# Softmax weights transposed by the DMA engines instead of TensorE, in a kernel of windowed attention and a feed-forward layer

## The chip, the cores and the metric

The program runs on one core of one Trainium2 chip. Five engines work side by side, each through its own list of instructions in order: TensorE (PE in the profile; its weight loads are PEld), VectorE (DVE), ScalarE (ACT), GpSimd (POOL) and SyncE (SP, which here does nothing but issue transfers). The metric is the device time of one execution in microseconds.

## The reference

Attention over a window of 128 positions with a linear bias by distance, for 8 batches of 8 heads, 576 positions and 64 elements a head; its output, one row of 512 for each of 4608 tokens, goes through a feed-forward layer of 2048 with an activation made of comparisons and a square.

```python
scores = scale * np.matmul(q, k.transpose(0, 1, 3, 2))
mask = (rel >= 0) & (rel < window)
scores = np.where(mask, scores + bias[None], -1000000000.0)
scores = scores - np.max(scores, axis=-1, keepdims=True)
attn = np.exp(scores)
attn = attn / (np.sum(attn, axis=-1, keepdims=True) + 1e-09)
return np.matmul(attn, v).astype(np.float32)
...
h = x @ w_in
g = np.where(pos, h, np.where(neg, 0.0, (h + beta) ** 2 / (4.0 * beta)))
return (g @ w_out).astype(np.float32)
```

## The kernel before

The 4608 tokens are cut into 12 chunks of 384 (CH), each of three blocks of 128. For each chunk the attention of 8 heads is done in 4 pairs, numbered p = 0 to 47 through the whole run, with heads m = 2p and 2p + 1. Then the feed-forward layer of that chunk runs in 16 steps, fc = 0 to 15. The attention of chunk c + 1 is woven into the feed-forward steps of chunk c, so that TensorE has matmuls of one while the other engines work on the other.

Products in float32 accuracy are made of float16 halves: a number is scaled, its rounded value is the high half, the rest the low half, and three matmuls (high by high, high by low, low by high) make one product. Chunks 0 and 1 are treated in plain float32 (LIGHT = 2), so 80 heads, in 40 pairs, take the path that the change touches.

A pair of heads passes these stages:

- scores_of_pair (L461) multiplies q and k on TensorE into PSUM banks named s_m_0 and s_m_2.
- soften adds the bias and takes the row maximum (L484, DVE), the exponential with its sums (L486, ACT), the sum's reciprocal (L493), folds the two window halves on each other (L497, DVE) and multiplies by the reciprocal (L498, DVE). The result ep_m is 128 queries by 384 (three blocks of 128 keys), float32, in SBUF. It has two buffers.
- weights_t turns each of the three blocks round, since the next matmul needs keys on the partitions: three float32 transposes on TensorE (L507) into a PSUM bank p_m. ACT writes the high half (L519) and DVE the low half (L520) from that bank into lu_m, which holds for each half six blocks of 128 by 128, the odd ones written here. POOL then makes of each odd block its part above and its part below the diagonal: L522 writes the even blocks, L524 rewrites the odd ones. lu has three buffers, so lu_m takes the place of lu_(m - 3), which the values of an earlier pair must have read.
- values_of_pair multiplies the weights of both heads with v (L564), 24 or 18 small matmuls into a bank x_p; L573 (ACT) and L574 (DVE) split the result into the halves that layer 1 reads.

The banks s, p and x share one pool of three PSUM banks (ps_a).

A feed-forward step is layer1 and layer2. layer1 makes 12 matmuls (L593 to L595) into a bank h; ACT makes u of it (L600), DVE makes g of u (L601) and of h (L602), ACT rounds g to gh (L609) and POOL subtracts for the low half gl (L610). layer2 runs two steps behind (LAG = 2), 9 matmuls (L625 to L627) into three banks acc; L627 reads gl. After step 15 ACT writes the rows out (L638) and SP stores them.

SP issues all transfers in order: the loads of q and k (L306, L307) and v (L379) of a pair, some five pairs ahead of their use, and the stores of the output.

The order on each engine isn't written out. The program hands the work to a scheduler in the order of a list of segments, in which for each pair stand: scores of p, the split of v, values of p - 1, weights_t(2p), the split of q and k of p + 1, weights_t(2p + 1). emit_attention spreads these over the half-steps of the feed-forward layer, and the scheduler then sets the order on every engine by its own reckoning of when each operand is ready and each buffer free.

Of the kernel before, what the change touches and what calls it, by code (L numbers as in the profile page):

```python
# [9 lines left out]
F16 = mybir.dt.float16  # L10
# [4 lines left out]
AF = mybir.ActivationFunctionType  # L15
ALU = mybir.AluOpType
# [4 lines left out]
def windowed_attention_then_ffn(  # L21
# [21 lines left out]
    V, S, G, T, DMA = nc.vector, nc.scalar, nc.gpsimd, nc.tensor, nc.sync  # L43
# [4 lines left out]
    P = 128  # L48
# [3 lines left out]
    NQB = 3  # L52
    CH = NQB * P
# [6 lines left out]
    TOP = 2.0 ** 14  # L60
# [8 lines left out]
    ap1 = ctx.enter_context(tc.tile_pool(name="ap1", bufs=1))  # L69
# [6 lines left out]
    def bank(name):  # L76
        return ps_a.tile([P, 4 * P], F32, name=name, tag="ps_a")


    ident = const.tile([P, P], F32, name="ident")  # L80
# [421 lines left out]
    def weights_t(m):  # L502

        ep = head[m]["ep"]
        pt = bank(f"p_{m}")[:, :CH].rearrange("r (i w) -> r i w", w=P)
        for i in range(NQB):
            T.transpose(pt[:, i, :], ep[:, i, :], ident)  # L507
        if m < LIGHT * H:
            lu = head[m]["lu"] = ap1.tile([P, 2 * NQB, P], F32, name=f"lu_{m}", tag="lu", bufs=3)
            own = lu[:, 1::2, :]  # L510
            ga = S.copy(own, pt)
            G.affine_select(out=lu[:, 0::2, :], in_=own, pattern=[[0, NQB], [-1, P]],
                            base=0, channel_multiplier=1, compare_op=ALU.is_gt, fill=0.0)
            gg = G.affine_select(out=own, in_=own, pattern=[[0, NQB], [1, P]],
                                 base=0, channel_multiplier=-1, compare_op=ALU.is_ge, fill=0.0)
            done_t[m] = [head[m]["held"].ins, ga.ins, gg.ins]
            return
        lu = head[m]["lu"] = ap1.tile([P, 2, 2 * NQB, P], F16, name=f"lu_{m}", tag="lu", bufs=3)
        ga = S.activation(lu[:, 0, 1::2, :], pt, AF.Copy, scale=TOP)  # L519
        gv = V.scalar_tensor_tensor(lu[:, 1, 1::2, :], pt, TOP, lu[:, 0, 1::2, :], ALU.mult, ALU.subtract)  # L520
        flat = lu.rearrange("p s i w -> p (s i) w")
        G.affine_select(out=flat[:, 0::2, :], in_=flat[:, 1::2, :], pattern=[[0, 2 * NQB], [-1, P]],  # L522
                        base=0, channel_multiplier=1, compare_op=ALU.is_gt, fill=0.0)
        gg = G.affine_select(out=flat[:, 1::2, :], in_=flat[:, 1::2, :], pattern=[[0, 2 * NQB], [1, P]],  # L524
                             base=0, channel_multiplier=-1, compare_op=ALU.is_ge, fill=0.0)
        done_t[m] = [ga.ins, gv.ins, gg.ins]
# [127 lines left out]
    def turn(m):  # L654
        segments.append([lambda: weights_t(m)])
        turned[m] = len(segments)
# [34 lines left out]
    for p in range(p8, NP):  # L691
        c, g = divmod(p, NPAIR)
        nc_, ng = divmod(p + 5, NPAIR)
        new = p + 5 < NP
        segments.append([lambda p=p: scores_of_pair(p, (0, 1))])
        if p == p8:
            segments.append([lambda p=p: behind(softened[p], lambda: reach_of(p + 4))])
        if new:
            segments.append([lambda p=p: behind(softened[p], lambda: reach_of(p + 5))])
        if new and ng == NPAIR - 1:  # L700
            segments.append([lambda nc_=nc_: level(nc_)])
        segments.append([lambda p=p: scores_of_pair(p, (2,))])
        if g == NPAIR - 1 and c + 1 < NCHUNK:
            segments.append([lambda c=c: near_of(c + 1)])
        segments.append([lambda p=p: split_v(p)] + ([lambda p=p: load_all(p + 6)] if p + 6 < NP else []))
        if p > p8:
            segments.append([lambda p=p: values_of_pair(p - 1)])
            if g == 0:
                ready.append(len(segments))
        if new and ng == NPAIR - 1:  # L710
            segments.append([lambda nc_=nc_: scale_all(nc_)])
        segments.append([lambda p=p: weights_t(2 * p)])
        if p + 1 < NP:
            segments.append([lambda p=p: split_qk(p + 1)])
        segments.append([lambda p=p: weights_t(2 * p + 1)])
# [98 lines left out]
    for i, ops in enumerate(ffn):  # L814
        c, r = divmod(i, STEPS)
# [37 lines left out]
```

## Time and profile before

| | |
|---|---|
| median of 3 runs | 983.93 us (983.66 to 986.0) |
| profiled execution | 983.55 us |
| span of the profiled execution | 981.8 us |
| mean granted TensorE clock | 0.989 of full |
| PE busy | 954.0 us, 97% |
| DVE, ACT, POOL busy | 74%, 62%, 36% |
| chain of work that ended last | PE 89%, DVE 4%, ACT 4%, DMA 1% |

The span runs from the first to the last instruction on the core; the execution's own time is 1.75 us longer. A busy PE is one whose matmuls overlap without a gap; since matmuls are pipelined, what one of them costs is read from the distance between the starts of two, not from the length of one. The granted clock is the share of full speed that TensorE had: 1.0 is 2.4 GHz, 0.5 is 1.2 GHz.

### The profile page before, as it was taken

To read this page: it belongs to the slowest core of one execution; us is meant where nothing else is said; L and a number is where in the kernel's file an instruction comes from. 1 tells how busy PE (TensorE), PEld (TensorE's weight loads), DVE (VectorE), ACT (ScalarE), POOL (GpSimd) and SP (SyncE) were. 2 spreads that over 40 slices of the span, in tenths; PEclk is the share of its full clock that TensorE was granted. 3 is DMA by queue.
4 is the path that set the end of the run, shared out by engine and by line. 5 is a ranking of instruction groups with operands and counts; after the bars stand their busy time and mean duration, and the time that the engine had idled before them with its cause. 6 is when DMAs were issued, how large, how long until landed. Compare 5 with 4: busy or idle time off the path is not lost.

```text
span 981.8 us, 17793 instructions
## 1 busy us (share of the span) xinstructions
PE 954.0 (97%) x6181; PEld 523.0 (53%) x6181; DVE 722.9 (74%) x2073; ACT 607.3 (62%) x1508; POOL 357.6 (36%) x464
## 2 busy tenths in 40 slices
PE   8699999998999999999999999999999999999998
PEld 5344545554555555555555555555555555555554
DVE  7888888887777886786786787687677786765332
ACT  6888767667557555666665765665666655544332
POOL 5322313334343334333434433533433443334221
PEclk9899999997999999999999999999999999999999
DMA  8557520021011111012111111112101000000000
GB/s 266 187 190 268 189 65 33 12 66 65 30 52 57 33 41 63 30 49 70 35 52 34 57 41 39 63 30 60 62 30 31 33 1 2 33 1 1 33 1 32
DMA packets 53289, 59.86 MB, mean 61 GB/s; under 512 B 3408, under 2 KB 42576, under 8 KB 53200
## 3 DMA queue, kind: packets, MB, share of 16 engines
q1 hardware_dynamic: 53056, 58.60, 18.6%
q8 instruction: 48, 0.79, 0.3%
q14 instruction: 41, 0.34, 0.1%
q10 hardware_dynamic: 144, 0.13, 0.0%
HBM read 49.28 MB, written 9.44 MB: 60 GB/s over the span
## 4 chain that ended last, share of the span: by engine, by line
PE 89%; DVE 4%; ACT 4%; DMA 1%; issue 1%; SPq 0%; POOL 0%; ACTq 0%; DVEq 0%; POOLq 0%
PE h L593 13%; PE h L595 12%; PE h L594 12%; PE acc L625 12%; PE acc L626 12%; PE acc L627 12%; PE s L461 5%; PE x L564 4%; PE p L507 3%; PE acc L622 3%; PE x L541 1%; ACT z L486 1%; ACT raw L183 1%; PE s L445 1%; DMA k<-in_k_dram 1%
## 5 line engine op out<-in xcount | busy, mean ns | idle before, releaser
L610 POOL TENSOR_TENSOR gl<-g,gh 128x384 f16<-128x384 f32 x176 | 167.6, 952 | 432.9 <-ACT gh L609 424.9
L601 DVE SCALAR_TENSOR_TENSOR g<-u,half 128x384 f32<-128x384 f32 x176 | 121.9, 693 | 156.8 <-ACT u L600 146.4
L609 ACT CAST gh<-g 128x384 f16<-128x384 f32 x176 | 89.6, 509 | 186.1 <-DVE g L602 104.3
L625 PE MATMUL acc<-wo,gh 128*128 128x512 f16 x528 | 200.3, 379 | 0.0
L626 PE MATMUL acc<-wo,gh 128*128 128x512 f16 x528 | 200.3, 379 | 0.0
L627 PE MATMUL acc<-wo,gl 128*128 128x512 f16 x528 | 196.5, 379 | 0.0
L600 ACT ACTIVATE u<-h,shift,fall 128x384 f32<-128x384 f32 x176 | 116.6, 665 | 99.8 <-PE h L595 99.6
L486 ACT ACTIVATE z<-z,nmax 128x256 f32<-128x256 f32 (+2 forms) x288 | 137.7, 480 | 35.0 <-DVE nmax L484 29.7
L593 PE MATMUL h<-x,wi 128*128 128x384 f16 x384 | 125.7, 329 | 3.1 <-DVE g L602 1.5
L593 PE MATMUL h<-xh,wi 128*128 128x384 f16 x384 | 124.8, 327 | 2.5 <-DVE g L602 2.5
L594 PE MATMUL h<-x,wi 128*128 128x384 f16 x384 | 126.0, 328 | 0.0
L595 PE MATMUL h<-x,wi 128*128 128x384 f16 x384 | 125.9, 328 | 0.0
L594 PE MATMUL h<-xl,wi 128*128 128x384 f16 x384 | 125.2, 326 | 0.0
L595 PE MATMUL h<-xh,wi 128*128 128x384 f16 x384 | 125.0, 326 | 0.0
L484 DVE CUSTOM_DVE_ANT_0 z<-s,near,z_of 128x256 f32<-128x256 f32 (+2 forms) x240 | 98.5, 460 | 33.8 <-PE s L461 33.6
L602 DVE SCALAR_TENSOR_TENSOR g<-h,gain,g 128x384 f32<-128x384 f32 x176 | 108.2, 615 | 3.9
L593 PEld LDWEIGHTS <-wi 128*128 128x128 f16 x768 | 75.1, 98 | 63.1 <-issue 7.1
L594 PEld LDWEIGHTS <-wi 128*128 128x128 f16 x768 | 75.3, 98 | 59.5 <-issue 7.3
L595 PEld LDWEIGHTS <-wi 128*128 128x128 f16 x768 | 75.2, 98 | 52.3 <-issue 4.0
L522 POOL TENSOR_SCALAR_AFFINE_SELECT lu<-lu 128x768 f16<-128x768 f16 x80 | 70.1, 890 | 64.1 <-DVE lu L520 63.7
L627 PEld LDWEIGHTS <-gl 128*128 128x128 f16 x528 | 51.5, 98 | 58.7 <-issue 0.4
L625 PEld LDWEIGHTS <-gh 128*128 128x128 f16 x528 | 51.6, 98 | 50.8 <-issue 0.8
(150 smaller groups left out, 1455.5 us busy)
## 6 DMA issues: line engine op xcount, KB each, us to landing
out_dram<-o SPq DMA_DIRECT2D x35, 256.0 KB, 2.1
raw<-in_moe_w_in_dram SPq DMA_DIRECT2D x16, 512.0 KB, 3.8
raw<-in_moe_w_out_dram SPq DMA_DIRECT2D x16, 512.0 KB, 4.7
vn<-in_v_dram SPq DMA_DIRECT2D x32, 256.0 KB, 2.8
qk<-in_q_dram SPq DMA_DIRECT2D x40, 192.0 KB, 2.4
qk<-in_k_dram SPq DMA_DIRECT2D x28, 256.0 KB, 2.8
vn<-in_v_dram SPq DMA_DIRECT2D x16, 192.0 KB, 2.6
qk<-in_k_dram SPq DMA_DIRECT2D x12, 192.0 KB, 2.6
```

The lines of the kernel that those rows point to most:

```text
L484: a = V.tensor_tensor_reduce(out=z[:, i, c0:], in0=pt[:, n, c0:], in1=r[:, c0:], op0=ALU.add, op1=ALU.min, scale=factor, scalar=3.0e38, ac ...
L486: b = S.activation(z[:, i, c0:], z[:, i, c0:], AF.Exp, bias=nmax[:, i:i + 1], scale=-1.0, accum_out=sm[:, i, 0:1])
L593: T.matmul(ph, wi[fc][:, 0, cc, :], xh, start=(cc == 0), stop=False)
L594: T.matmul(ph, wi[fc][:, 0, cc, :], xl, start=False, stop=False)
L595: T.matmul(ph, wi[fc][:, 1, cc, :], xh, start=False, stop=(cc == NCC - 1))
L600: first = S.activation(u, ph, AF.Relu, bias=shift[c] if c else quarter, scale=fall[c][:, col])
L601: V.scalar_tensor_tensor(g, u, half[c] if c else 0.5, u, ALU.min, ALU.mult)
L602: last = V.scalar_tensor_tensor(g, ph, gain[c][:, col] if c else fall[c][:, col], g, ALU.mult, ALU.max)
L610: G.tensor_tensor(gl, g, gh, ALU.subtract)
L625: T.matmul(a, gh[:, ts], wo[fc][:, 0], start=first, stop=False)
L626: T.matmul(a, gh[:, ts], wo[fc][:, 1], start=False, stop=False)
L627: T.matmul(a, gl[:, ts], wo[fc][:, 0], start=False, stop=last)
```

## The change

From chunk 2 on, weights_t splits ep_m where it stands: ACT writes the high half and DVE the low half into a new tile hl_m (128 queries by two halves by 384 keys, float16, two buffers). One transfer on SP's queue with a transpose, 128 x 768 elements, 192 KB, turns the six 128 x 128 blocks round and writes them into the odd blocks of lu_m. POOL's two instructions are as before. The three TensorE transposes and the bank p_m are gone from these heads; chunks 0 and 1 keep them.

```diff
--- before.py
+++ after.py
@@ -502,10 +502,10 @@
     def weights_t(m):
 
         ep = head[m]["ep"]
-        pt = bank(f"p_{m}")[:, :CH].rearrange("r (i w) -> r i w", w=P)
-        for i in range(NQB):
-            T.transpose(pt[:, i, :], ep[:, i, :], ident)
         if m < LIGHT * H:
+            pt = bank(f"p_{m}")[:, :CH].rearrange("r (i w) -> r i w", w=P)
+            for i in range(NQB):
+                T.transpose(pt[:, i, :], ep[:, i, :], ident)
             lu = head[m]["lu"] = ap1.tile([P, 2 * NQB, P], F32, name=f"lu_{m}", tag="lu", bufs=3)
             own = lu[:, 1::2, :]
             ga = S.copy(own, pt)
@@ -516,9 +516,11 @@
             done_t[m] = [head[m]["held"].ins, ga.ins, gg.ins]
             return
         lu = head[m]["lu"] = ap1.tile([P, 2, 2 * NQB, P], F16, name=f"lu_{m}", tag="lu", bufs=3)
-        ga = S.activation(lu[:, 0, 1::2, :], pt, AF.Copy, scale=TOP)
-        gv = V.scalar_tensor_tensor(lu[:, 1, 1::2, :], pt, TOP, lu[:, 0, 1::2, :], ALU.mult, ALU.subtract)
+        hl = ap1.tile([P, 2, NQB, P], F16, name=f"hl_{m}", tag="hl", bufs=2)
+        ga = S.activation(hl[:, 0], ep, AF.Copy, scale=TOP)
+        gv = V.scalar_tensor_tensor(hl[:, 1], ep, TOP, hl[:, 0], ALU.mult, ALU.subtract)
         flat = lu.rearrange("p s i w -> p (s i) w")
+        DMA.dma_start(flat[:, 1::2, :], hl.rearrange("p s i w -> p (s i w)"), transpose=True)
         G.affine_select(out=flat[:, 0::2, :], in_=flat[:, 1::2, :], pattern=[[0, 2 * NQB], [-1, P]],
                         base=0, channel_multiplier=1, compare_op=ALU.is_gt, fill=0.0)
         gg = G.affine_select(out=flat[:, 1::2, :], in_=flat[:, 1::2, :], pattern=[[0, 2 * NQB], [1, P]],
```

Lines behind weights_t are two higher in the changed kernel: L600 to L602 are L602 to L604 there, L610 is L612, L564 is L566; in weights_t itself L522 and L524 become L524 and L526.

The scheduler places the work anew. Three places show it. In the names, the number behind a head, pair or step is a running number of the tile.

POOL, around pair 22 (heads 44 and 45, chunk 5), which is woven into the feed-forward layer of chunk 4. gl_4_6 is the low half of g in step 6 of chunk 4. Before:

```order
L610 TENSOR_TENSOR gl_4_6_5147<-g_4_6_5142,gh_4_6_5146 128x384
L610 TENSOR_TENSOR gl_4_7_5220<-g_4_7_5215,gh_4_7_5219 128x384
L610 TENSOR_TENSOR gl_4_8_5265<-g_4_8_5260,gh_4_8_5264 128x384
L610 TENSOR_TENSOR gl_4_9_5333<-g_4_9_5328,gh_4_9_5332 128x384
L522 AFFINE_SELECT lu_44_5227<-lu_44_5227 128x6x128
L522 AFFINE_SELECT lu_45_5272<-lu_45_5272 128x6x128
L524 AFFINE_SELECT lu_44_5227<-lu_44_5227 128x6x128
L524 AFFINE_SELECT lu_45_5272<-lu_45_5272 128x6x128
L610 TENSOR_TENSOR gl_4_10_5393<-g_4_10_5388,gh_4_10_5392 128x384
```

and now:

```order
L612 TENSOR_TENSOR gl_4_5_5031<-g_4_5_5026,gh_4_5_5030 128x384
L612 TENSOR_TENSOR gl_4_6_5091<-g_4_6_5086,gh_4_6_5090 128x384
L524 AFFINE_SELECT lu_44_5167<-lu_44_5167 128x6x128
L526 AFFINE_SELECT lu_44_5167<-lu_44_5167 128x6x128
L524 AFFINE_SELECT lu_45_5210<-lu_45_5210 128x6x128
L526 AFFINE_SELECT lu_45_5210<-lu_45_5210 128x6x128
L612 TENSOR_TENSOR gl_4_7_5164<-g_4_7_5159,gh_4_7_5163 128x384
L612 TENSOR_TENSOR gl_4_8_5207<-g_4_8_5202,gh_4_8_5206 128x384
```

The pair's four selects stood behind gl of step 9; now they stand behind gl of step 6, and gl of step 7 stands behind them.

DVE, the same pair. Before, the low halves stood behind both parts of g of step 9:

```order
L602 SCALAR_TENSOR_TENSOR g_4_9_5328<-h_4_9_5314,gain4_4708,g_4_9_5328 128x384
L369 SCALAR_TENSOR_TENSOR h_24_5481<-qk_12_1544,s_k6_5060,h_24_5481 128x384
L520 SCALAR_TENSOR_TENSOR lu_44_5227<-p_44_5223,lu_44_5227 128x3x128
L520 SCALAR_TENSOR_TENSOR lu_45_5272<-p_45_5268,lu_45_5272 128x3x128
L601 SCALAR_TENSOR_TENSOR g_4_10_5388<-u_4_10_5387,half4_4710 128x384
L602 SCALAR_TENSOR_TENSOR g_4_10_5388<-h_4_10_5374,gain4_4708,g_4_10_5388 128x384
```

and now the two low halves follow their ep at once:

```order
L498 TENSOR_TENSOR ep_44_4952<-z_44_4953,rc_44_5044 128x384
L498 TENSOR_TENSOR ep_45_4959<-z_45_4960,rc_45_5051 128x384
L603 SCALAR_TENSOR_TENSOR g_4_6_5086<-u_4_6_5085,half4_4660 128x384
L521 SCALAR_TENSOR_TENSOR hl_44_5168<-ep_44_4952,hl_44_5168 128x384
L604 SCALAR_TENSOR_TENSOR g_4_6_5086<-h_4_6_5072,gain4_4658,g_4_6_5086 128x384
L521 SCALAR_TENSOR_TENSOR hl_45_5211<-ep_45_4959,hl_45_5211 128x384
```

They moved up by three steps, between and behind the two parts of g of step 6.

PE, the last pair of chunk 2 (pair 11, heads 22 and 23). Before, the transposes, the scores of the next pair and the values of pair 11 followed one another, after the last layer-1 matmul for which there was an input (x_2_3, the output of pair 11, is still missing to h_2_0 and h_2_1):

```order
L595 MATMUL h_2_1_2823<-x_2_2_2473,wi1_565 128x384
L507 MATMUL p_22_2476<-ident_85,ep_22_2331 128x128 x3
L507 MATMUL p_23_2524<-ident_85,ep_23_2338 128x128 x3
L461 LDWEIGHTS h_12_2510
L461 MATMUL s_25_0_2558<-h_12_2510 128x128
...
L461 MATMUL s_24_2_2597<-h_12_2510 128x256
L564 LDWEIGHTS vs_11_2432
L564 MATMUL x_11_2651<-lu_22_2480,vs_11_2432 64x256
L564 LDWEIGHTS vs_11_2432
L564 MATMUL x_11_2651<-lu_23_2528,vs_11_2432 64x256
```

and now:

```order
L597 MATMUL h_1_15_2679<-x_1_1_1163,wi15_1472 128x384
L566 LDWEIGHTS vs_11_2420
L566 MATMUL x_11_2635<-lu_22_2464,vs_11_2420 64x256
L595 LDWEIGHTS wi15_1472
L595 MATMUL h_1_15_2679<-x_1_2_1373,wi15_1472 128x384
...
L627 MATMUL acc_1_2_1814<-wo6_2493,gh_1_13_2535 128x512
L628 LDWEIGHTS gh_1_13_2535
L628 MATMUL acc_1_2_1814<-wo6_2493,gh_1_13_2535 128x512
L566 LDWEIGHTS vs_11_2420
L566 MATMUL x_11_2635<-lu_23_2510,vs_11_2420 64x256
```

The values of pair 11 moved up among layer 1 of step 15 and layer 2 of step 13 of chunk 1, and nothing of the pair but scores and values is left on PE.

## Rows read from the trace of the kernel before

**Rows 1.** The page's section 1: busy time, share of the span, instructions of each engine.

```profile
PE 954.0 (97%) x6181; PEld 523.0 (53%) x6181; DVE 722.9 (74%) x2073; ACT 607.3 (62%) x1508; POOL 357.6 (36%) x464
```

**Rows 2.** PE's timeline, 505 to 530 us: start, length, engine, line, operation, count.

```profile
509.34 1.01 PE L564 MATMUL x<-lu,vs 128*64 128x256 f16 x18
...
514.52 0.33 PE L594 MATMUL h<-xl,wi 128*128 128x384 f16 x1
514.68 0.33 PE L595 MATMUL h<-xh,wi 128*128 128x384 f16 x1
514.84 0.38 PE L625 MATMUL acc<-wo,gh 128*128 128x512 f16 x1
515.06 0.38 PE L626 MATMUL acc<-wo,gh 128*128 128x512 f16 x1
...
516.78 0.82 PE L507 MATMUL p<-ident,ep 128*128 128x128 f32 x6
517.53 0.28 PE L461 MATMUL s<-h 64*128 64x256 f16 x1
...
522.56 0.82 PE L461 MATMUL s<-h 64*128 64x256 f16 x12
```

**Rows 3.** Whom PE waited for, 200 to 260 us: total us, times, longest.

```profile
PE h L593 <- ACT x L573: 1.1, 1, 1.1
PE x L564 <- POOL lu L524: 1.0, 2, 0.6
PE s L461 <- DVE nmax L484: 0.8, 1, 0.8
PE s L461 <- DVE lu L520: 0.7, 1, 0.7
PE h L593 <- DVE g L602: 0.5, 1, 0.5
```

**Rows 4.** Stretches of 5 us: busy us of PE, PEld, DVE, ACT, POOL; PEclk; DMA.

```profile
220.00:225.00 5.00, 2.52 (x28) 1.62 (x27) 4.04 (x16) 3.13 (x12) 3.31 (x4) 0.86 0.52 191
225.00:230.00 5.00, 3.91 (x29) 2.76 (x29) 3.87 (x14) 3.87 (x13) 0.00 (x0) 0.50 0.27 92
230.00:235.00 5.00, 4.48 (x21) 2.60 (x19) 3.59 (x7) 3.05 (x6) 2.18 (x3) 0.61 0.18 52
```

**Rows 5.** Single lines, whole run: ns min/median/max, first and last start, shapes.

```profile
L519 ACT ACTIVATE lu<-p x80: 469/486/514, 159.3 to 901.9; 128x384 f16<-128x384 f32 x80
L520 DVE SCALAR_TENSOR_TENSOR lu<-p,lu x80: 541/549/559, 161.2 to 902.4; 128x384 f16<-128x384 f32 x80
L368 ACT ACTIVATE h<-qk,s_q x40: 598/615/626, 128.5 to 853.7; 128x384 f16<-128x384 f32 x40
L369 DVE SCALAR_TENSOR_TENSOR h<-qk,s_q,h x40: 605/615/1284, 130.1 to 854.4; 128x384 f16<-128x384 f32 x40
L524 POOL TENSOR_SCALAR_AFFINE_SELECT lu<-lu x80: 855/862/1356, 163.1 to 904.5; 128x768 f16<-128x768 f16 x80
```

**Rows 6.** Timelines of ACT, DVE and POOL from 515 us: one layer-1 block's way.

```profile
515.04 0.67 ACT L600 ACTIVATE u<-h,shift,fall 128x384 f32<-128x384 f32 x1 [1.84 <-PE h L595]
...
515.82 0.62 DVE L601 SCALAR_TENSOR_TENSOR g<-u,half 128x384 f32<-128x384 f32 x1
516.47 0.62 DVE L602 SCALAR_TENSOR_TENSOR g<-h,gain,g 128x384 f32<-128x384 f32 x1
...
517.77 0.91 POOL L610 TENSOR_TENSOR gl<-g,gh 128x384 f16<-128x384 f32 x1 [0.29 <-ACT gh L609]
```

**Rows 7.** DMA: issues (KB, us to landing); a queue's packets, MB, share; landings of qk.

```profile
qk<-in_q_dram SPq DMA_DIRECT2D x40, 192.0 KB, 2.4
...
k<-in_k_dram SPq DMA_DIRECT2D x4, 192.0 KB, 5.3
...
q1 hardware_dynamic: 53056, 58.60, 18.6%
...
DMA to landing us min/median/max: 2.3/2.4/4.3
```

## The prediction

> **What bounds the kernel now.** I read the page's busy shares first: PE is busy for 954.0 of 981.8 us, DVE for 74%, ACT for 62%, POOL for 36% [rows 1]. A kernel whose TensorE is at 97% gains by what is taken off TensorE, as long as the others keep up. Next I read PE's timeline in the steady part [rows 2]. The starts follow each other without a gap: a layer-1 matmul starts 0.16 us after the one before (514.52, 514.68, 514.84), a layer-2 matmul 0.22 us after (514.84, 515.06), where the whole difference is the size of the tile. So here PE is a list of matmuls whose prices add up, and other engines matter only where PE waits for them. Such waits are few behind chunk 1, but one place stands out: between 220 and 235 us PE waited five kinds of times, 1.1 + 1.0 + 0.8 + 0.7 + 0.5 = 4.1 us [rows 3], and the granted clock was 0.86, 0.50 and 0.61 in these three stretches of 5 us [rows 4], that is 1.2 GHz for most of it.
>
> **What leaves PE.** 40 pairs lose six transposes each. From the first transpose of a pair at 516.78 to the next matmul at 517.53 is 0.75 us [rows 2]; 40 x 0.75 = 30.0 us. All of it is on the bounding engine with nothing beside it, so the full 30.0 counts, if nothing arrives late in its place.
>
> **What leaves with the waits.** At 220 us the chain was: transposes of pair 11, split by ACT and DVE, selects by POOL, values of pair 11, split of x, layer 1 of chunk 2. As the first order rows of PE in the section on the change show, nothing but scores stood between the transposes and the values; layer 1 had no other input to go on with, and the scores even waited for a bank that DVE was still reading (s L461 <- DVE lu L520) [rows 3]. In the new order the values stand among steps 13 to 15 of chunk 1, and no p bank is in the pool. Between the layer-1 step behind which DVE splits head 22 and the values I count 30 layer-1, 27 layer-2 and 18 score matmuls, about 11.6 us at the spacings of [rows 2], where before there were scores alone. I take the stall as gone. Its price: 4.1 us of waits, and the time at a low clock, busy time by the missing share: 2.52 x 0.14 + 3.91 x 0.50 + 4.48 x 0.39 = 4.1 us [rows 4]. Together 8.2 us.
>
> **What is added to ACT and DVE.** The splits read SBUF instead of PSUM. Those from PSUM took 0.486 and 0.549 us; the same shape from SBUF, in the split of q, took 0.615 on both [rows 5]. That is 80 x 0.13 = 10 us more on ACT and 80 x 0.07 = 5 us on DVE, on engines with a quarter of their time free [rows 1]: nothing on the path. If they were on it, 15 us.
>
> **What the transfer costs.** No transpose by DMA is in this trace. From below: a load of the same 192 KB takes 2.4 us from issue to landing [rows 7]. From above: the same size took 4.3 us at worst among the loads of q and k in mid-run, and 5.3 us at the crowded start [rows 7]. Farther up by packets: queue 1 moved 53056 packets in 18.6% of 16 engines' span, 0.186 x 981.8 x 16 / 53056 = 55 ns a packet of 1.1 KB on average. At that, 192 KB of a load are 178 packets, 11 on each of the 16 engines, 0.6 us, which leaves 1.8 us that hangs on no packet. If a transpose moves rows of one block (128 elements, 256 bytes), it has 768 packets, 48 an engine, 2.6 us, and lands after 1.8 + 2.6 = 4.4 us. In pieces of 128 bytes it would be 7.1 us, in pieces of 32 bytes 23 us. I take 4.4 us, an estimate, being close to the rows of this size (2.4 to 5.3); 2.4 and 23 stay as ends.
>
> The Trainium skill speaks on both sides. VectorE: DVE Perf Modes, section The three transpose paths, gives 1309 ns for a 128 x 128 block by DMA against 390 ns on TensorE, and its rules for kernel authors prefer TensorE where the result may go to PSUM; here a block on TensorE takes 0.125 us of the path in a row of six. Six blocks at 1309 ns would be 7.9 us a transfer, an estimate from that page, which is the first rival below. Advanced Engine Details and Errata, section X-Bar Transpose (TRN2), says that such DMAs are as fast as ordinary ones; by that it would be 2.4 us, and the forecast stands.
>
> **Who waits for it.** POOL's first select of a head now waits for the landing instead of for DVE. Behind it on POOL stand the head's other select and gl of the next feed-forward step, and PE needs that gl (L627, now L629). Take pair 22, whose four selects all stand ahead of gl_4_7. Time zero is the end of the last matmul of h_4_6. By the way of one block [rows 6], u is ready at 0.7, g's first part at 1.4; with a split of 0.615 between the parts, as the new order of DVE has it, hl_44 is ready at 2.0, g's second part at 2.6, hl_45 at 3.2. After the second landing come two selects of 0.862 [rows 5], gl of 0.91 [rows 6] and about 0.1 of signals: 2.7 us. On PE stand until the first L629 on gl_4_7, counted in the new order: the values of pair 21 (24 at 0.053, from 18 in some 0.95 us), two sets of nine and one of two layer-2 matmuls more (2 + 9 + 9 + 9 = 29 at 0.215), three layer-1 steps (36 at 0.1625), 13 scores (0.8) [rows 2]: 1.3 + 6.2 + 5.9 + 0.8 = 14.2, less 0.2 for the end of the first, 14.0 us. So the second transfer may land until 14.0 - 2.7 = 11.3. If the two transfers run at once, that allows 8.1 us each; if strictly one after the other from 2.0 on, (11.3 - 2.0) / 2 = 4.65 us each. At 4.4 both hold, the second barely. The values have more room: 15.6 to 19.9 us from such a zero in most pairs, 11 in chunk 2 and in the last pair, where they need 3.2 + 4.4 + 1.8 = 9.4.
>
> SP's queue: a transpose waits there for DVE's low half, for POOL, and for the values of the pair before, since lu_45 takes the place of lu_42; loads for pairs five or six ahead and stores of output are queued behind. A pair takes about 18 us on PE, so a load that starts some us later still lands long before its use: nothing. The issue itself is on an engine that does nothing else.
>
> **Sum.** 983.55 - 30.0 - 8.2 = 945.4. Behind chunk 1 PE's waits outside the stall are short, 0.5 to 1.4 us like those of [rows 3]; the new order is as likely to make some as to lose some, and with the second landing so near its limit I add 3.5 us: 948.9. The profiled run lies 0.38 us under the median, so 949.3; I say 949.
>
> **The rivals.** A change of 0.3%, 3 us, is about what a measurement of this kernel can tell from none.
>
> First, the transfers are slow and follow one another, and POOL's queue hands the lateness to PE. Against it: loads of this size land in 2.4 us and the DMA engines are mostly idle in mid-run, queue 1 taking 18.6% [rows 7]. For it: pieces are surely smaller than those of a load. It decides from 4.65 us a transfer. At 7.1 us the second lands at 2.0 + 14.2 = 16.2, 4.9 late; ten of the 40 pairs have all four selects ahead of one gl with such a limit, 49 us; in the other 30 the values come at 17.7 and need 16.2 + 1.8 = 18.0, 0.3 late, 9 us. Waits cost as much again by the clock where it falls as in [rows 4], so 949 + 58 to 949 + 116; I price it at 1035 us. At 23 us a transfer two need 46 us in a pair's 18, and the run would be 1700 us or more. The Trainium skill's 1309 ns a block, above, lies in this case, if the transfers don't overlap.
>
> Between: at 5.5 us one after the other the second is 1.7 us late in ten pairs, 17 us, or twice that with the clock: 966 to 983.
>
> Second, the transfers are in time, but the order made by the scheduler brings back what the stall gave, and where DVE is fullest (the first two chunks of the new path) PE's gain of 8 x 0.75 = 6 us turns into waits: 949 + 8 + 6 = 963. For it: DVE at 74% overall is one engine with little slack in places. Against it: the new order gives longer distances than the old.
>
> That the change doesn't take the transposes off PE is excluded: in its order these heads have no L507 left.
>
> **How the numbers follow.** Forecast, 942 to 956: 0.62. Second rival, 956 to 972: 0.15. Between, 972 to 990: 0.06. First rival, above 990: 0.17. Faster by over 0.3% is 0.62 + 0.15 and half of the 0.06: 0.80. Within 0.3%: 0.03. Slower: 0.17. The range that leaves out no more than 0.2 is 940 (no wait added, none of the old left) to 990.
>
> **What would show it.** PE's L508 only 48 times, all before 160 us. PE at full clock between 200 and 240 us, without the five waits. Landing of the transposes at about 4.4 us, the second of a pair no later than 8 us behind its split. PE's waits for POOL gl or lu under 5 us in total; if they are tens of us, the first rival holds. If waits for DVE or ACT grow, the second. The prediction is wrong if the transpose lands after 5 us and its neighbour follows only then.

## The result, and the profile after

The changed kernel takes 962.5 us (median of 4 runs, 961.1 to 964.0) where the kernel before, beside it on the same chip, took 984.6 (983.7 to 986.0): ratio 0.9775, interval 0.9754 to 0.9795. It is faster, and the time lies in the range; but 949 was forecast, and of the 34.7 us of gain in the sum 21.4 came (983.55 to 962.11 in the profiled runs). The place of the loss and nearly its size are those of the second rival, which named 963 us.

The page's section 1 of after, to set beside [rows 1]:

```profile
PE 936.4 (98%) x5941; PEld 490.1 (51%) x5941; DVE 762.6 (79%) x2073; ACT 604.0 (63%) x1508; POOL 381.5 (40%) x464
```

PE has 240 instructions fewer, as the change says. DVE has as many as before and is busy 39.7 us longer; POOL, whose work wasn't touched, 23.9 us longer. The next rows are the new path: the transpose issues (line, engine, operation, count: ns min/median/max, first and last start), their landing, queue 1, and the two splits that now read SBUF. They answer to [rows 5] and [rows 7].

```profile
L523 SPq DMA_TRANSPOSE lu<-hl x80: 1209/1216/2104, 161.6 to 875.8; - x80
DMA to landing us min/median/max: 2.7/2.8/4.9
q1 hardware_dynamic: 117056, 74.34, 28.7%
L520 ACT ACTIVATE hl<-ep x80: 509/523/530, 157.8 to 874.2; 128x384 f16<-128x384 f32 x80
L521 DVE SCALAR_TENSOR_TENSOR hl<-ep,hl x80: 537/545/1064, 161.0 to 874.9; 128x384 f16<-128x384 f32 x80
```

A transfer lands after 2.8 us, less than the 4.4 estimated; the splits take 0.523 and 0.545 us, less than the 0.615 they were costed at. So neither of the two things that the change adds explains what is missing.

To see where it is missing I cut both profiled runs at the first output of chunks 0, 3 and 9 (first ACT activation into o; 148.0, 383.9, 842.0 us before, 148.8, 381.2, 823.8 after). A dozen or two matmuls change sides at a cut (from chunk 0 to 3 after has 18 scores and 5 full matmuls more than before, and the later stretches as many fewer), so a difference holds to some 1.5 us.

| stretch | before | after | gain | transposes that left | gain in the sum |
|---|---|---|---|---|---|
| start to chunk 0's output | 148.0 | 148.8 | -0.8 | 0 | 0 |
| chunk 0 to 3 | 235.9 | 232.4 | 3.5 | 72 | 72 x 0.125 + 8.2 = 17.2 |
| chunk 3 to 9 | 458.1 | 442.6 | 15.5 | 144 | 18.0 |
| chunk 9 to the end | 139.8 | 136.5 | 3.3 | 24 | 3.0 |

Of the 16.7 us missing before the allowance of 3.5, 13.7 are missing between chunk 0 and 3, 2.5 in the steady part. The early stretch first. Whom PE waited for from 140 to 260 us in after (total us, times, longest):

```profile
PE h L595 <- DVE g L604: 2.8, 2, 2.0
PE x L566 <- POOL lu L526: 1.2, 1, 1.2
PE x L566 <- DVE i_q L328: 1.0, 1, 1.0
PE s L461 <- DVE nmax L484: 0.3, 1, 0.3
PE s L461 <- DVE i L346: 0.2, 1, 0.2
```

These are 5.5 us, where the stall of [rows 3] had 4.1; from chunk 0 to 3 PE's idle time is 5.7 us, and was 5.5. DVE ends most of these waits. The same 120 us by engine (busy us of PE, PEld, DVE, ACT, POOL; PEclk; DMA), first in the kernel before, then in after, and after's two slices behind the longest wait, as in [rows 4]:

```profile
140.00:260.00 120.00, 115.92 (x754) 63.31 (x753) 97.47 (x273) 81.96 (x212) 44.07 (x47) 0.96 0.14 44
```

```profile
140.00:260.00 120.00, 114.45 (x743) 59.12 (x742) 114.68 (x297) 84.95 (x223) 47.60 (x47) 0.97 0.27 67
200.00:205.00 5.00, 4.33 (x37) 2.71 (x37) 4.37 (x13) 4.15 (x13) 0.91 (x1) 0.63 0.20 54
205.00:210.00 5.00, 5.00 (x20) 2.25 (x19) 4.85 (x15) 5.00 (x14) 0.91 (x1) 0.68 0.25 53
```

DVE was busy 97.5 of 120 us and is now busy 114.7. After the waits PE's granted clock was again between its two levels, 0.63 and 0.68 of 2.4 GHz in two slices of 5 us. Which of the two sets the time, DVE or the clock, shows in a run described below, bunch, which adds matmuls to the last chunk alone: its order is that of after on every engine up to 890 us. Its window and its largest wait of PE there (L599 and L613 are L595 and L604 of after):

```profile
140.00:260.00 120.00, 111.94 (x744) 57.89 (x743) 114.68 (x297) 84.45 (x222) 48.21 (x47) 1.00 0.27 67
PE h L599 <- DVE g L613: 4.5, 3, 2.0
```

The clock was full, DVE was busy for the same 114.7 us, and chunk 0 to 3 took the same 232 us (232.3, after 232.4): PE waited 8.0 us there instead of 5.7. So here DVE is the bound: at the faster clock PE only waited longer. The chain of waits points the same way for the whole run; its first line by engine, of before and of after:

```profile
PE 89%; DVE 4%; ACT 4%; DMA 1%; issue 1%; SPq 0%; POOL 0%; ACTq 0%; DVEq 0%; POOLq 0%
```

```profile
PE 78%; DVE 12%; ACT 6%; issue 2%; DMA 1%; POOL 0%; SPq 0%; DVEq 0%; ACTq 0%; POOLq 0%
```

Why DVE is fuller shows at the longest wait. After's timelines of PE, DVE and POOL around 198 us (start, length, engine, line, operation; in brackets the idle time before and who ended it):

```profile
197.95 0.38 PE L629 MATMUL acc<-wo,gl 128*128 128x512 f16 x1
200.32 0.32 PE L595 MATMUL h<-x,wi 128*128 128x384 f16 x1 [1.99 <-DVE g L604]
```

```profile
196.31 1.04 DVE L428 SCALAR_TENSOR_TENSOR vs<-vn,s,vs 128x384 f16<-128x384 f32 x1
...
197.33 1.15 DVE L369 SCALAR_TENSOR_TENSOR h<-qk,s_k,h 128x384 f16<-128x384 f32 x1
...
198.48 1.14 DVE L603 SCALAR_TENSOR_TENSOR g<-u,half 128x384 f32<-128x384 f32 x1
199.65 0.62 DVE L604 SCALAR_TENSOR_TENSOR g<-h,gain,g 128x384 f32<-128x384 f32 x1
```

```profile
194.37 0.86 POOL L524 TENSOR_SCALAR_AFFINE_SELECT lu<-lu 128x768 f16<-128x768 f16 x1 [4.13 <-DMA lu<-hl]
195.21 0.92 POOL L612 TENSOR_TENSOR gl<-g,gh 128x384 f16<-128x384 f32 x1
196.07 0.86 POOL L526 TENSOR_SCALAR_AFFINE_SELECT lu<-lu 128x768 f16<-128x768 f16 x1
196.89 1.18 POOL L524 TENSOR_SCALAR_AFFINE_SELECT lu<-lu 128x768 f16<-128x768 f16 x1
198.14 1.06 POOL L526 TENSOR_SCALAR_AFFINE_SELECT lu<-lu 128x768 f16<-128x768 f16 x1
```

PE waits 1.99 us for g. Ahead of it DVE ran three instructions that take about 0.6 us each when POOL stands still (shortest L428: 0.583) and took 1.04, 1.15 and 1.14, 1.5 us more, while POOL, released by a landing, ran five in a row. Sorted over the whole of after by whether a POOL instruction overlaps, L603 takes 0.608 us without (93 times) and 0.917 with one (83), the split of k in 512 columns (L369) 0.741 (15) and 1.111 (13); L604, whose h comes from PSUM, takes 0.613 either way. Before, 55 of 176 of L601 had such an overlap, and 4 of 28 of these splits of k.

Taken for every DVE instruction of the window from 140 to 260 us, what it lasts beyond the median of its kind without POOL beside it adds up to 3.5 us before and 15.9 us in after. The 24 instructions that DVE has more there take 7.4 us at those medians. Together that is 19.7 us, for 17.2 us more of busy time, since neighbouring records overlap at their ends. So most of the added load is lengthening and not more work. The groups of DVE over the whole run (busy, mean ns of one), before and after:

```profile
L601 DVE SCALAR_TENSOR_TENSOR g<-u,half 128x384 f32<-128x384 f32 x176 | 121.9, 693 | 156.8 <-ACT u L600 146.4 <-POOL lu L524 5.7 <-POOL gl L610 2.5
L369 DVE SCALAR_TENSOR_TENSOR h<-qk,s_k,h 128x384 f16<-128x384 f32 x12 | 7.5, 626 | 0.0
```

```profile
L603 DVE SCALAR_TENSOR_TENSOR g<-u,half 128x384 f32<-128x384 f32 x176 | 132.7, 754 | 136.2 <-ACT u L602 133.8 <-POOL lu L526 1.9
L369 DVE SCALAR_TENSOR_TENSOR h<-qk,s_k,h 128x384 f16<-128x384 f32 x12 | 10.2, 852 | 0.0
```

The Trainium skill (SBUF — State Buffer, section SBUF: two separate sides) says that a DVE instruction with two SBUF inputs and a GpSimd instruction that reads SBUF exclude each other. The times above agree with it, and so do those of L604, which has one input in PSUM.

### The profile page after: what moved, and what is told of

The parts are those of the page before. It is cut to its first block, busy times and chain, and to the rows that moved or that the text cites. A ratio compares the mean times of both kernels' runs of the same rounds, so it can differ in the third digit from the quotient of the medians.

```text
span 960.3 us, 17643 instructions
## 1 busy us (share of the span) xinstructions
PE 936.4 (98%) x5941; PEld 490.1 (51%) x5941; DVE 762.6 (79%) x2073; ACT 604.0 (63%) x1508; POOL 381.5 (40%) x464
## 4 chain that ended last, share of the span: by engine, by line
PE 78%; DVE 12%; ACT 6%; issue 2%; DMA 1%; POOL 0%; SPq 0%; DVEq 0%; ACTq 0%; POOLq 0%
PE h L595 12%; PE acc L627 11%; PE h L596 11%; PE h L597 11%; PE acc L628 10%; PE acc L629 10%; PE s L461 5%; PE x L566 4%; ACT z L486 2%; PE acc L624 2%; DVE g L603 2%; DVE z L484 1%; DVE g L604 1%; DVE h L369 1%; PE s L445 1%
## 5 line engine op out<-in xcount | busy, mean ns | idle before, releaser
L612 POOL TENSOR_TENSOR gl<-g,gh 128x384 f16<-128x384 f32 x176 | 185.1, 1052 | 383.8 <-ACT gh L611 367.9
L603 DVE SCALAR_TENSOR_TENSOR g<-u,half 128x384 f32<-128x384 f32 x176 | 132.7, 754 | 136.2 <-ACT u L602 133.8
L629 PE MATMUL acc<-wo,gl 128*128 128x512 f16 x528 | 199.3, 380 | 0.0
L602 ACT ACTIVATE u<-h,shift,fall 128x384 f32<-128x384 f32 x176 | 116.6, 663 | 46.1 <-PE h L597 45.7
L595 PE MATMUL h<-x,wi 128*128 128x384 f16 x384 | 126.0, 328 | 3.4 <-DVE g L604 3.0
L595 PE MATMUL h<-xh,wi 128*128 128x384 f16 x384 | 125.4, 327 | 1.1 <-DVE g L604 1.1
L604 DVE SCALAR_TENSOR_TENSOR g<-h,gain,g 128x384 f32<-128x384 f32 x176 | 107.9, 613 | 3.0
L595 PEld LDWEIGHTS <-wi 128*128 128x128 f16 x768 | 75.0, 98 | 64.9 <-issue 12.3
L524 POOL TENSOR_SCALAR_AFFINE_SELECT lu<-lu 128x768 f16<-128x768 f16 x80 | 74.7, 934 | 83.6 <-DMA lu<-hl 83.4
```

What stands on the lines that cost most here:

```text
L595: T.matmul(ph, wi[fc][:, 0, cc, :], xh, start=(cc == 0), stop=False)
L602: first = S.activation(u, ph, AF.Relu, bias=shift[c] if c else quarter, scale=fall[c][:, col])
L603: V.scalar_tensor_tensor(g, u, half[c] if c else 0.5, u, ALU.min, ALU.mult)
L604: last = V.scalar_tensor_tensor(g, ph, gain[c][:, col] if c else fall[c][:, col], g, ALU.mult, ALU.max)
L612: G.tensor_tensor(gl, g, gh, ALU.subtract)
L629: T.matmul(a, gl[:, ts], wo[fc][:, 0], start=False, stop=last)
```

## The experiments

Two theories were tested first. A: DVE is what PE waits for in the early stretch, and the transfer is hidden. B: the transfer and what it does to POOL's queue cost the time. Later runs test what in the steady part costs 2.5 us. Each edit is shown against the changed kernel; ratios are against the kernel before on the same chip. The scheduler places the work anew for each edit.

**The transfer taken out.** The halves go straight into the weights' tile, untransposed, so the transfer's work is left out.

```diff
-        ga = S.activation(hl[:, 0], ep, AF.Copy, scale=TOP)
-        gv = V.scalar_tensor_tensor(hl[:, 1], ep, TOP, hl[:, 0], ALU.mult, ALU.subtract)
-        DMA.dma_start(flat[:, 1::2, :], hl.rearrange("p s i w -> p (s i w)"), transpose=True)
+        ga = S.activation(lu[:, 0, 1::2, :], ep, AF.Copy, scale=TOP)
+        gv = V.scalar_tensor_tensor(lu[:, 1, 1::2, :], ep, TOP, lu[:, 0, 1::2, :], ALU.mult, ALU.subtract)
```

> The transfer is left out: ACT and DVE write the two halves straight into the odd blocks of the weights tile, so the weights are not turned round and the output is not the reference's; everything else stays. Theory A (between 150 and 240 us DVE is full, 114.7 busy of 120 us from 140 to 260, and PE waits for DVE; in the steady part PE pays about 0.095 us for each change of matmul shape, and the new order has more of them; the transfer itself is hidden): within 3 us of the changed kernel, 959 to 965 us. Theory B (the shortfall against 949 is lateness of the transfer, which POOL's queue hands on: POOL waited 83 us for landings): 950 us or less, with PE's waits between 140 and 260 us gone.

960.2 us, ratio 0.9754 (0.9736 to 0.9772), at the lower end of the interval of the change itself. From chunk 0 to 3 it takes 231.5 us (after 232.4), PE is idle for 6.5 us there, and DVE is busy 115.2 of the 120 us from 140 on, with its instructions lengthened by 16.3 us there. So the lengthening doesn't come from the transfers' traffic, and all transfers together cost some 2 us, if anything: the two intervals overlap. B falls.

**A part of DVE's work taken away.** The low half, which DVE also wrote before the change, becomes a second copy by ACT, so its value is left out.

```diff
-        gv = V.scalar_tensor_tensor(hl[:, 1], ep, TOP, hl[:, 0], ALU.mult, ALU.subtract)
+        gv = S.activation(hl[:, 1], ep, AF.Copy, scale=TOP)
```

> The low half of the weights is not computed: ACT writes a second copy of the high half instead, so DVE loses 80 instructions of 0.55 us (44 us) and ACT gains 42; the output is less exact than the reference's. Theory A: the 11 us or so of waits and low clock between 150 and 240 us mostly go, 953 to 957 us, and the steady part (380 to 820 us) stays as it is, 73.8 us a chunk. Theory B: 960 to 964 us, since the landing is as late as before.

956.8 us, ratio 0.9724 (0.9706 to 0.9741). The 5 us come from the early stretch: chunk 0 to 3 takes 226.4 us, chunk 3 to 9 442.3, as in after (442.6). Its window and its only wait of PE for this path from 140 to 260 us:

```profile
140.00:260.00 120.00, 116.94 (x773) 60.23 (x771) 110.71 (x302) 93.12 (x243) 50.86 (x51) 1.00 0.34 75
```

```profile
PE x L566 <- POOL lu L526: 2.5, 2, 1.9
```

DVE is 4 us less busy, PE's waits for it are gone, and the clock is full; the clock alone would not have helped, as bunch shows. A holds for the early stretch: in the steady part the same 0.545 us a head cost nothing, here they cost 6 us. That shows DVE to be the bound here; it doesn't make the low half a new load.

**POOL's share of the selects taken away.** If POOL's instructions lengthen DVE's, fewer on POOL should free DVE. The first select becomes a copy on ACT, so its mask is left out.

```diff
-        G.affine_select(out=flat[:, 0::2, :], in_=flat[:, 1::2, :], pattern=[[0, 2 * NQB], [-1, P]],
-                        base=0, channel_multiplier=1, compare_op=ALU.is_gt, fill=0.0)
+        S.copy(flat[:, 0::2, :], flat[:, 1::2, :])
```

> POOL's first select of each head is replaced by a plain copy on ACT, without its mask, so the output is not the reference's. POOL loses 75 us, ACT gains some 65. Theory A with the sharing of DVE and POOL (an L603 takes 0.60 us alone and 0.85 to 0.96 us when a POOL instruction overlaps it): DVE's busy time falls by 10 to 20 us of its 763, the waits between 150 and 240 us shrink, 955 to 960 us. If DVE's longer instructions come from the transfers' writes instead, DVE's busy time stays at 763 us and the time at 962.

A miss, by 40 us: 1001.8, ratio 1.0181 (1.0158 to 1.0204). DVE's busy time did fall by 26.0 us, to 736.6, and POOL's by 84.6. But the wait for the landing came to ACT. Its row, the answering row of POOL in after, and PE's largest wait:

```profile
ACT lu L524 <- DMA lu<-hl: 83.4, 59, 3.9
PE h L594 <- DVE g L603: 20.1, 21, 2.4
```

```profile
POOL lu L524 <- DMA lu<-hl: 83.4, 44, 4.6
```

83.4 us of waiting for the same transfer are hidden on POOL; with them on ACT the run is some 40 us longer. A likely way is that u of the next layer-1 step stands behind the waiting copy, and PE needs g, which DVE makes from u. ACT also has 58 us more to do, and what of the 40 us is the waiting and what the copies wasn't separated. As a test of what POOL does to DVE's share of PE's waits the run is spoiled; only the 26 us of DVE's busy time speak: they agree with A, and the transfers were still there.

**How much cover the transfer has.** Every transfer is done two or three times into the same place.

```diff
-        DMA.dma_start(flat[:, 1::2, :], hl.rearrange("p s i w -> p (s i w)"), transpose=True)
+        for i in range(2):
+            DMA.dma_start(flat[:, 1::2, :], hl.rearrange("p s i w -> p (s i w)"), transpose=True)
```

> Every transposing transfer is made twice, the second into the same place after the first has landed; the result is the same. The landing, 2.8 us in the changed kernel with 1.2 us of issue, becomes some 5.6 us or more. By the budget of the prediction the second head of a pair may land until 8.1 us behind its split; two heads at twice the transfer land about 2.8 + 1.2 + 2.8 + 2.8 = 9.6 us behind the first split, 11.6 on the clock whose limit is 11.3: theory A expects next to nothing, 961 to 966 us. Theory B (lateness already costs in the changed kernel): each us more costs, 975 us or more.

> Every transposing transfer is made three times in a row into the same place. The second head lands some 15 us behind the first split, 17 on a clock whose limit is 11.3, if the order were the same; the scheduler knows of the added transfers and may set the selects later. Theory A: this is past the cover, PE's waits for POOL rise to tens of us and the time to 980 to 1060 us. If even this stays under 970, the cover is wider than the budget of the prediction says. Theory B: far above 1000 us.

Twice: 966.8 us, ratio 0.9826 (0.9810 to 0.9843), 5 us over after, with 443.9 us from chunk 3 to 9. Three times: 1002.5, ratio 1.0201 (1.0180 to 1.0223), 471.8 us there. PE's waits, first of two transfers, then of three:

```profile
PE x L567 <- POOL lu L527: 8.0, 5, 3.9
```

```profile
PE x L567 <- POOL lu L527: 24.3, 22, 2.5
PE acc L630 <- POOL gl L613: 6.1, 9, 1.6
```

The repeats don't wait for each other's landing, as the expectation had it. Each lands 2.8 us behind its issue, but one follows the other after 1.4 us; three issues in the run with three, of which the first lands at 921.73:

```profile
918.95 4.01 SPq L524 DMA_TRANSPOSE lu<-hl  x3
```

So the last landing of a pair comes 4.6 us behind the end of its first split in after, 7.7 with two transfers and 11.1 with three (medians of 40 pairs; the longest are 7.2, 11.3 and 15.2). In steady chunks a second transfer is hidden (the rest of the 5 us is in the early stretch, 236.2 instead of 232.4), a third isn't. The limit that the prediction counted, 11.3 - 2.0 = 9.3 us behind the first split, lies between the two. With three it comes out where the first rival said, in values and in gl, but most of it in the values, which the rival had nearly in time.

**Chunk 2 alone, and all but chunk 2.** The choice of DMA or TensorE is made by the head's number; one half of the edit is shown, the other heads keep the old lines.

```diff
-        if m < LIGHT * H:
+        by_dma = m >= (LIGHT + 1) * H
+        if not by_dma:
             pt = bank(f"p_{m}")[:, :CH].rearrange("r (i w) -> r i w", w=P)
```

> Chunk 2's eight heads go back to TensorE's transposes; the DMA transpose begins with chunk 3. Theory A: the four pairs cost 2.9 us of PE again, and the old stall of 8 to 9 us takes the place of the new one of about the same size, so 962 to 967 us. If the change in chunk 2 had given what was forecast (3 us of PE and 8 us of stall), 973 us.

> Only chunk 2's eight heads are transposed by DMA; from chunk 3 on TensorE does it as in the kernel before. Theory A: one stall gives way to another and 2.9 us of PE are gained, 979 to 985 us. As forecast before the result (3 us of PE and 8 us of stall gained): 973 us.

From chunk 3 on: 966.9 us, ratio 0.9827 (0.9806 to 0.9847). Chunk 2 alone (LIGHT * H <= m < (LIGHT + 1) * H): 978.9, ratio 0.9952 (0.9937 to 0.9967). The gains of 17.0 and 4.7 us add up to the change's 22 us. So chunk 2 is worth 4.7 us, not its transposes and the stall, 3.0 + 8.2 = 11.2; the other 36 pairs 17.0, not 27.0. Without chunk 2 the early stretch is 237.8 us, longer than before the change, although fewer transposes stand in it, and PE's largest wait from 140 to 400 us is

```profile
PE x L572 <- POOL lu L532: 5.7, 3, 4.6
```

Each order has its own stall in this place. Chunk 2 alone has one too (2.0 us for g, 1.6 for lu, 1.0 for i_q).

**What a change of tile shape costs on PE.** With no wait left from 380 to 820 us, the steady part was still 2.5 us short. In before the values mostly followed scores at once (23 of 24 pairs from chunk 3 to 9), in after once; there PE changes between 128 x 128 tiles, scores (64 rows) and values (64 columns) 201 times instead of 171. Three kernels put the same 60 extra matmuls into the last chunk: 64 rows, in a bunch; 64 rows, one behind each three of layer 1; 128 rows, one behind each three.

```diff
-            T.matmul(ph, wi[fc][:, 1, cc, :], xh, start=False, stop=(cc == NCC - 1))
+            at_ = T.matmul(ph, wi[fc][:, 1, cc, :], xh, start=False, stop=(cc == NCC - 1))
+            if c == NCHUNK - 1 and fc > 0:
+                for _ in range(1):
+                    r = lo_rows[0]
+                    behind([at_.ins] + extra[-1:], lambda: extra.append(T.matmul(
+                        spare[0][:, :P], wi[0][r, 0, 0, :], xs[c][0][0][r, :P], start=True, stop=True, skip_group_check=True).ins))
```

For the bunch the range is 60 at one place (fc == 1, cc == 1) and 0 elsewhere; for 128 rows the whole partition range stands for r.

> 60 matmuls of 64 rows (128 columns) into a spare bank are added to the last chunk's layer 1, where there is no attention left, all in one row at step 1. Their result is not used. Each costs 0.05 to 0.11 us: 3 to 7 us more than the changed kernel, 965 to 969 us. It is the base for the next two.

> The same 60 matmuls of 64 rows, but one behind each group of three layer-1 matmuls in steps 1 to 15 of the last chunk, so that PE changes shape 120 times instead of twice. Theory A: 118 x 0.095 = 11 us more than with all in a row, 974 to 980 us. If a change of shape costs nothing: the same as in a row within 2 us.

> As the spread of 60, but with all 128 rows, so that they interrupt layer 1 at the same 60 places without a change of shape. Theory A: 60 x 0.055 = 3.3 us more than the changed kernel, 964 to 968 us, and some 9 us less than the spread of narrow ones. If the interruption itself costs, as much as the spread of narrow ones.

Bunch 966.9 us, ratio 0.9822 (0.9804 to 0.9841); spread 977.9, 0.9936 (0.9921 to 0.9950); full 966.8, 0.9820 (0.9803 to 0.9836). Spread less bunch is 11.0 us for 118 more changes, 0.093 us each; full, at the same places and no longer than bunch, shows that the interruption alone costs nothing. PE's timeline, spread, then full:

```profile
905.38 0.33 PE L601 MATMUL h<-xh,wi 128*128 128x384 f16 x1
905.64 0.23 PE L605 MATMUL spare<-xh,wi 64*128 64x128 f16 x1
905.79 0.34 PE L599 MATMUL h<-xh,wi 128*128 128x384 f16 x1
```

```profile
906.54 0.33 PE L601 MATMUL h<-xh,wi 128*128 128x384 f16 x1
906.71 0.22 PE L605 MATMUL spare<-xh,wi 128*128 128x128 f16 x1
906.76 0.33 PE L599 MATMUL h<-xh,wi 128*128 128x384 f16 x1
```

The steps are 0.26 and 0.15 us with 64 rows, 0.17 and 0.05 with 128: one change in, one out, with no gap marked as waiting.

**Values beside scores again.** If changes cost, the values put just ahead of the next pair's last scores should give some back.

```diff
-        segments.append([lambda p=p: scores_of_pair(p, (2,))])
+        segments.append(([lambda p=p: values_of_pair(p - 1)] if p > p8 else []) + [lambda p=p: scores_of_pair(p, (2,))])
+        if p > p8 and g == 0:
+            ready.append(len(segments))
...
-        if p > p8:
-            segments.append([lambda p=p: values_of_pair(p - 1)])
-            if g == 0:
-                ready.append(len(segments))
```

> The changed kernel with the values of pair p - 1 put directly ahead of the last scores of pair p in the list, in one segment with them, so that both groups of narrow matmuls stand together on PE. Its order has 289 changes between kinds of matmul from chunk 3 on, where the changed kernel has 315 and the kernel before 275. Theory A at 0.095 us a change: 26 x 0.095 = 2.5 us less, 958 to 962 us. If a change of shape costs nothing, 962 us, or more where the values now come before their weights are ready.

A miss: 969.1 us, ratio 0.9855 (0.9835 to 0.9876). The changes fell (289 instead of 315 in the program's order), but PE's waits grew, also those of the values for their weights. Over the whole run:

```profile
PE h L595 <- DVE g L604: 7.0, 5, 5.2
PE x L566 <- POOL lu L526: 5.7, 8, 1.3
```

Twenty-six changes are worth 2.4 us; the waits cost more. From chunk 3 to 9 it takes 445.2 us, of which PE is idle for 3.3; from chunk 0 to 3 PE is idle for 11.4 us.

**DVE relieved in the early stretch, nothing left out.** In chunk 1 DVE also makes the low halves of the output weights (L238). POOL, busy there for 47.6 of 120 us, takes them.

```diff
-        S.activation(t[:, 0], f, AF.Copy, scale=s_out)
-        V.scalar_tensor_tensor(t[:, 1], f, s_out, t[:, 0], ALU.mult, ALU.subtract)
+        S.mul(f, f, s_out)
+        S.copy(t[:, 0], f)
+        G.tensor_tensor(t[:, 1], f, t[:, 0], ALU.subtract)
```

> A correct version made from theory A. In chunk 1, where DVE is full, the low halves of the output weights (16 instructions L238 of 0.76 us on DVE) are made by POOL instead, from a weight tile that ACT scales in place first (16 more ACT instructions of about 0.7 us). DVE loses 12 us between 150 and 230 us; POOL, busy for 48 of 120 us there, gains 20, which lengthens some DVE instructions by 0.25 to 0.35 us where they overlap. Theory A: 956 to 960 us, all of the gain before 380 us. If POOL's queue, with its waits for landings, hands the weights on too late, or the sharing eats the gain, 962 us or more.

961.1 us (959.9 to 962.3), ratio 0.9767 (0.9746 to 0.9788): not to be told from after's 0.9775. From chunk 0 to 3 it takes 230.0 us, 2.4 less than after, and DVE is down to 110.88 of 120 us, but there PE now waits for POOL:

```profile
PE x L567 <- POOL lu L527: 3.1, 3, 1.4
PE acc L630 <- POOL gl L613: 2.3, 4, 0.9
```

Some of the wait moved from DVE to POOL, and the stretch up to chunk 0's output takes 151.1 us after 148.8, so that nothing is left of the gain. No kernel that computes the reference was measured clearly faster than the changed one.

## Why the prediction was right and wrong

**What leaves PE: right, the price a little too high.** 240 transposes are gone; L508 runs 48 times, the last at 124.0 us. But the row of six from which 0.125 us was read ends in a change to 64-row scores. A row of six that a layer-2 matmul follows, in the kernel before:

```profile
572.36 0.82 PE L507 MATMUL p<-ident,ep 128*128 128x128 f32 x6
573.01 0.38 PE L625 MATMUL acc<-wo,gh 128*128 128x512 f16 x1
```

That is 0.65 us, 0.109 us each, so the term is 240 x 0.109 = 26.2 us and not 30.0. The 0.10 us between 0.75 and 0.65 is one change of shape, which the new order pays in another place.

**What leaves with the waits: wrong, and the largest miss.** "I take the stall as gone", 8.2 us. From 220 to 235 us only one wait of 0.8 us, for g, is left of the kinds in [rows 3]. But PE is idle from chunk 0 to 3 for 5.7 us instead of 5.5, and the clock fell there too, for 4.33 x 0.37 + 5.00 x 0.32 = 3.2 us instead of 4.1. Idle time and clock together are 5.7 + 3.2 = 8.9 us and were 5.5 + 4.1 = 9.6: of the 8.2 us 0.7 came. In bunch, at full clock, the 8.0 us of waits alone are nearly as much. Counting matmuls between the values and their inputs told only that this one wait would go. What I didn't do was ask which engine is next late there. The bound I named for the second rival, "where DVE is fullest", could be read from the window from 140 to 260: 97.5 of 120 us, when I argued with the 74% of the whole run.

**What is added to ACT and DVE: right in size, wrong in "nothing on the path".** The splits are cheaper than costed. But in the early stretch DVE's load went up by 17.2 us, of two kinds: 24 instructions more in the window, since attention work now runs earlier (chunk 1's first output comes 17 us later, at 234.8 instead of 217.9, and chunk 3's 2.7 earlier), and, for the larger part, instructions lengthened beside POOL's, 15.9 us instead of 3.5. The prediction had no term for either. The run without the low half on DVE shows that DVE's load binds there: taking them off gives 6 us back. What a run without the lengthening would give isn't shown, as the run meant for it moved a wait to ACT.

**What the transfer costs: right that it is hidden, too high in size.** 2.8 us against the estimate of 4.4. The packets were nearly as estimated: queue 1 has 64000 more, 800 a transfer, where 768 rows of 256 bytes were counted. What was wrong is the cost of a packet taken from loads: by the queue's shares, 0.287 of 960.3 us against 0.186 of 981.8, times 16 engines, the added packets took 23 ns each and not 55. The 4.3 us read as the worst load of this size was a load of 256 KB; of 192 KB it was 4.0, which changes nothing. Of the Trainium skill's two pages, Advanced Engine Details and Errata, section X-Bar Transpose (TRN2), comes nearer (2.8 us beside 2.4 for a load of that size); 1309 ns a block from VectorE: DVE Perf Modes, section The three transpose paths, would have been 7.9 us, an estimate.

**Who waits for it: right.** The transfers of a pair run side by side: in 38 of 40 pairs the second is issued before the first has landed, and the second lands 3.6 us behind its split (median), where 8.1 were allowed. The limit holds: a second transfer each time costs the steady part 1.3 us, a third 29. From 160 us on PE waits 1.2 us for POOL's lu and not at all for gl. The first rival is out; the run with three transfers is what it would have looked like.

**The allowance of 3.5 us: right in size for the steady part's lack, wrong in kind.** There are no waits from 380 to 820 us, where PE is busy throughout. What is there is the price of the transposes, 144 x 0.016 = 2.3 us too high, and shape changes, 201 instead of 171 from chunk 3 to 9: 30 x 0.093 = 2.8 us. They were in no term. The trace of before could have priced them: between 390 and 810 us the step from a layer-1 matmul to scores is 0.26 us there (median of 33), to the next of layer 1 0.16, and [rows 2] names the shapes of both. 144 x 0.109 = 15.7 us of transposes, 1.6 of PE's idle time that is gone, some 1.2 for the 10 matmuls that fall on the other side of the cuts, less 2.8 make 15.7; 15.5 were measured.

PE's time in the early stretch then adds up so: of the 13.7 us missing there, 8.2 - 0.7 = 7.5 are the stall that came back in another place, 1.2 the price of 72 transposes, 26 more shape changes are 2.4, and 18 score and 5 full matmuls more fall into the stretch, 18 x 0.06 + 5 x 0.2 = 2.1 (13 scores take 0.8 us). 0.5 us stays open, less than the cut is good for. This says where PE's time went; since DVE binds there, PE's share could shrink without a gain. Why the scheduler's order puts more of the attention into chunk 1 wasn't tried.

**The rivals.** The second was right: gain turned into waits in the first two chunks of the new path, DVE the one waited for, 963 us priced, 962.5 measured. That the price is so near is partly luck: its 8 + 6 us stand against 13.7 missing there, of which some 6 are shape changes, matmuls that moved and the price of the transposes, and the allowance of 3.5 hides the 2.5 of the steady part. It got 0.15 with "Against it: the new order gives longer distances than the old", an argument on one wait, where the mechanism was DVE's load.

## What to carry to other kernels

A stall that a change removes is a gain only as far as the next engine in that same stretch allows: read the busy times of the stretch, not of the run, before taking it as gone. Before moving work that waits for a transfer to another engine, look at what is queued behind it there: 83 us of waiting were hidden on POOL, and the run that put them, with 58 us of copies, on ACT was 40 us longer. Read the price of a row of matmuls from one that is followed by the same tile shape. When matmuls of other tile shapes are strewn among full ones, count the changes of shape as work on TensorE.

## What was not expected of the hardware

- A change of tile shape on PE between 128 x 128 and 64-row tiles costs 0.093 us (11.0 us for 118 changes between two kernels with the same 60 added matmuls).
- DVE instructions with SBUF inputs take 0.608 us alone and 0.917 beside POOL's (L603), up to 1.33; with an input in PSUM (L604) 0.613 either way. Five POOL instructions in a row behind one landing lengthened three of DVE's by 1.5 us, and PE waited 2.0 us behind them.
- A DMA transpose of 192 KB from SBUF to SBUF lands in 2.8 us, though it keeps SP 1.21 us for its issue; the next on the queue is issued 1.4 us later (median) and lands some 1.6 us later. Two for each head are hidden here and three aren't.
